# Expert weights laid out by unit, each unit shifted against the moving tiles

## The chip, the cores and the metric

The kernel runs on one core of a Trainium2 chip. The metric is the device time of one execution in microseconds (us). Two runs of the kernel before took 2676.49 and 2677.51 us, median 2677.0. A third execution was profiled; it took 2676.21 us, of which the traced span is 2674.3.

## The reference

Three stages follow each other, all in float32. First, a long convolution: for 2 batches of 12,480 positions and 128 channels, `u = x * v` is convolved along the sequence with a filter that a small network makes from the position embedding (through real FFTs of twice the length), and the result is multiplied by `x`. Its output, 24,960 tokens of 128 channels, then goes through two dense blocks, which the kernel calls experts:

```python
h = x @ w_in                                  # 128 -> 2048
x = (h * np.cos(h)) @ w_out                   # first,  2048 -> 128
h = x @ w_in2
y = (h * np.clip(h + 3, 0, 6) / 6) @ w_out2   # second
```

The expert weights arrive as float64. The kernel decodes each into two float32r numbers, a high and a low part.

## The kernel before, in words

`conv_phase` computes the convolution with two short Fourier transforms as matmuls, in some 530 us. Beside it two `decoder` lanes fetch and decode the expert weights: 16 tasks of 512 columns, four for each of the weight matrices `wi`, `wo` (first expert, in or out) and `vi`, `vo` (second). A task loads 64-bit words by a DMA from SyncE, splits exponent and mantissa on VectorE and ScalarE, writes the high part with a ScalarE copy (L129) and the low part with a GpSimd product (L136). The conv stage calls `step_decode` once in each of its 64 steps, so a task is spread over several steps.

`moe_phase` runs both experts, from about 530 us to the end. Tokens come in 49 tiles of 512 columns (448 in the first and the last). The 2048 hidden channels are cut into 8 units of 256. For each tile and unit:

- `front` (L701 is its operand line, L700 its call) makes the hidden values of one unit: for each of two halves of 128 channels three matmuls are added up in PSUM, high weight by high token, high weight by low token, low weight by high token. These are six matmuls, with one unit's weights as the stationary operand and a token tile (`xh`, `xl`, or `x2h`, `x2l` for the second expert) as the moving one.
- `m1_reduce`, `m1_gate`, `m1_split` (first expert) or `m2_gate`, `m2_split` (second) apply the nonlinearity on ScalarE and VectorE and split the result into `hi` and `lo`; the last subtraction is on GpSimd (L733, L758).
- `back` (L768) multiplies by the output weights, six matmuls again, and adds into `acc`. After the eighth unit `acc` becomes the next expert's token tile or the output.

The loop over `p` at the end of `moe_phase` writes the order out by hand. In its steady part one position issues `front` of the first expert, `back` of the first expert's unit three positions earlier, `front` of the second expert and `back` of its unit three positions earlier: 24 matmuls in four runs of six, each run with the weights of one unit. The units of the four runs differ. `tc.manual_schedule()` keeps this order on every engine. Before the loop 12 matmuls into `busy` (L791) keep TensorE occupied.

Where the tiles lie matters for the change. In the kernel before, a weight tile of the first expert is 128 x 2 x 2048 float32r, all high parts and then all low parts: 16,384 bytes in a partition. A tile of the second expert has `HB` = 4160 elements, 16,640 bytes, since the convolution uses the same place before it. `HB` and `XB` are rounded up to `LINE` = 64 elements, 256 bytes. Moving tiles are 1,792, 2,048 or 4,096 bytes. All of these are multiples of 256 bytes, so every weight tile and every moving tile begins at the same place within 256 bytes, and each stationary block (128 columns, 512 bytes) does too.

Of the kernel before, what the change touches and what calls it, by code (L numbers as in the profile page):

```python
# [9 lines left out]
FP32 = mybir.dt.float32  # L10
F32R = mybir.dt.float32r
# [3 lines left out]
ALU = mybir.AluOpType  # L15
# [13 lines left out]
MP = 2 * M2  # L29
# [4 lines left out]
DFF = 2048  # L34
KFF = DFF // 128
TOK = B * S
TT = 512
XW = 4 * N2
LINE = 64
HB = -(-max(36 * MP, 2 * DFF) // LINE) * LINE  # L40
XB = -(-XW // LINE) * LINE
TILES = [(TT + TOK % TT) // 2] + [TT] * (TOK // TT - 1) + [(TT + TOK % TT) // 2]
TWO_PI = 2.0 * np.pi
# [3 lines left out]
def kernel(  # L47
# [19 lines left out]
    nc = tc.nc  # L67
    dram = ctx.enter_context(tc.tile_pool(name="dram", bufs=1, space=DRAM))
    wp = ctx.enter_context(tc.tile_pool(name="wp", bufs=1))
    scr = dram.tile([D, B, NP1 * N2], FP32, name="scr")  # L70

    w_hi = {}
    w_lo = {}
    DC = 512

    hq = ctx.enter_context(tc.tile_pool(name="hq", bufs=1))

    def weights(e, nm):
        if (nm, e) not in w_hi:
            if e == 0:  # L80
                t = wp.tile([128, 2, DFF], F32R, name=f"w{nm}")
            else:
                t = hq.tile([128, HB], F32R, tag=f"h{'io'.index(nm)}", name=f"v{nm}")[:, :2 * DFF]
                t = t.rearrange("p (z f) -> p z f", f=DFF)
            w_hi[nm, e], w_lo[nm, e] = t[:, 0, :], t[:, 1, :]
        return w_hi[nm, e], w_lo[nm, e]

    b_exp = wp.tile([128, 1], FP32, name="b_exp")
# [9 lines left out]
    def fetch(task, pool, lane):  # L98
# [9 lines left out]
            )  # L108
        return st

    def decode(task, st, pool, lane):
        e, nm, c = task
        lo, hi = st[:, :, 0], st[:, :, 1]
        ex = pool.tile([128, DC], INT32, tag=f"wex{lane}", name="wex")
        mh = pool.tile([128, DC], INT32, tag=f"wmh{lane}", name="wmh")
        m = mh.bitcast(FP32)
        wh, wl = (w[:, c:c + DC] for w in weights(e, nm))
        nc.vector.tensor_scalar(ex, hi, 9, 0x3FFFFF, op0=ALU.logical_shift_right, op1=ALU.bitwise_and)
        nc.vector.tensor_scalar(mh, hi, 0x1FF, None, op0=ALU.bitwise_and)
        yield  # L120
        nc.scalar.activation(out=ex, in_=ex, func=ACTF.Relu, bias=b_exp, scale=-1.0)
        nc.scalar.activation(out=ex, in_=ex, func=ACTF.Relu, bias=b_max, scale=-(2.0 ** 12))
        nc.scalar.activation(out=m, in_=mh, func=ACTF.Copy, scale=2.0 ** -20)
        yield
        nc.vector.scalar_tensor_tensor(
            out=ex, in0=hi, scalar=-0x80000000, in1=ex, op0=ALU.bitwise_and, op1=ALU.bitwise_or
        )
        yield
        nc.scalar.copy(wh, ex.bitcast(FP32))  # L129
        nc.vector.scalar_tensor_tensor(  # L130
            out=m, in0=lo.bitcast(UINT32), scalar=2.0 ** -52, in1=m, op0=ALU.mult, op1=ALU.add
        )
        yield
        nc.vector.tensor_scalar(ex, ex, -0x800000, None, op0=ALU.bitwise_and)
        yield
        nc.gpsimd.tensor_tensor(out=wl, in0=m, in1=ex.bitcast(FP32), op=ALU.mult)  # L136

    LANES = 2
    order = [(0, nm, c) for c in range(0, DFF, DC) for nm in "io"] + [(1, nm, c) for nm in "io" for c in range(0, DFF, DC)]
# [1 line left out]
    def decoder(lane, pool):  # L141
        tasks = order[lane::LANES]
        for _ in range((0, 3)[lane]):
            yield
        st = fetch(tasks[0], pool, lane)
        yield
        for k, task in enumerate(tasks):
            for j, _ in enumerate(decode(task, st, pool, lane)):
                if j == 4 and k + 1 < len(tasks):
                    st = fetch(tasks[k + 1], pool, lane)  # L150
                yield
            yield
# [481 lines left out]
    def moe_phase(mctx):  # L634
# [14 lines left out]
        acc = {}  # L649

        def n_of(t):
            return TILES[t]

        def load_x(t):
            if t >= NT:
                return
            n = n_of(t)
            if t == 0 and n <= XW and _runs(0, n) == [[0, 0, n]]:
                xf[t] = x0_t[t]
                return  # L660
            f = x_p.tile([128, TT], FP32, tag="xf", name="xf")
            done = 0
            for b, p, step in _runs(starts[t], n):
                nc.sync.dma_start(out=f[:, done:done + step], in_=scr[:, b, p:p + step])
                done += step
            xf[t] = f
# [18 lines left out]
        def front(e, t, u, split):  # L685
            n = n_of(t)
            un = Unit()
            un.e, un.t, un.u, un.n = e, t, u, n
            xh, xl = xs[e, t]
            if split:  # L690
                hs = [ps_a.tile([128, 1, TT], FP32, tag=f"ha{c}", name=f"ha{c}") for c in range(2)]
                un.parts = [(slice(c, c + 1), hs[c][:, :, :n]) for c in range(2)]
            else:
                h = ps_b.tile([128, 2, TT], FP32, tag="hb", name="hb")
                hs = [h[:, c:c + 1] for c in range(2)]
                un.parts = [(slice(0, 2), h[:, :, :n])]
            for c in range(2):
                sl = slice((2 * u + c) * 128, (2 * u + c + 1) * 128)
                for k, (w, r) in enumerate(((w_hi, xh), (w_hi, xl), (w_lo, xh))):
                    nc.tensor.matmul(  # L700
                        out=hs[c][:, 0, :n], lhsT=w["i", e][:, sl], rhs=r[:, :n], start=(k == 0), stop=(k == 2)  # L701
                    )
            return un

# [55 lines left out]
        def back(un):  # L760
            e, t, u, n = un.e, un.t, un.u, un.n
            if u == 0:
                bank = 1 if t == 0 else e
                acc[e] = ps_o.tile([128, TT], FP32, tag=f"acc{bank}", name=f"acc{e}")
            for k, (w, r) in enumerate(((w_hi, un.hi), (w_lo, un.hi), (w_hi, un.lo))):
                for c in range(2):
                    sl = slice((2 * u + c) * 128, (2 * u + c + 1) * 128)
                    nc.tensor.matmul(  # L768
                        out=acc[e][:, :n], lhsT=w["o", e][:, sl], rhs=r[:, c, :n],
                        start=(u == 0 and c == 0 and k == 0), stop=(u == KFF // 2 - 1 and c == 1 and k == 2),  # L770
                    )
            if u == KFF // 2 - 1:
                a = acc[e][:, :n]
                if e == 0:
                    hi = x2_p.tile([128, TT], F32R, tag="x2h", name="x2h")
                    lo = x2_p.tile([128, TT], F32R, tag="x2l", name="x2l")
                    nc.scalar.copy(hi[:, :n], a)
                    nc.vector.tensor_tensor(out=lo[:, :n], in0=a, in1=hi[:, :n], op=ALU.subtract)
                    xs[1, t] = (hi, lo)
                else:  # L780
                    o = o_p.tile([128, TT], FP32, tag="o", name="o")
                    nc.scalar.activation(out=o[:, :n], in_=a, func=ACTF.Copy, scale=1.0 / 6.0)
                    nc.sync.dma_start(out=out_t[:, starts[t]:starts[t] + n], in_=o[:, :n])
# [4 lines left out]
        first, second = {}, {}  # L788
        busy = ps_o.tile([128, TT], FP32, tag="acc0", name="busy")
        for _ in range(12):  # L790
            nc.tensor.matmul(out=busy, lhsT=w_hi["i", 0][:, :128], rhs=w_hi["i", 0][:, :TT])  # L791
        load_x(0)
        load_x(1)
        split_x(0)
        for p in range(P2 + 3):
            if p < P1:
                t, u = divmod(p, NU)
                un = first[p] = front(0, t, u, p >= SHIFT or p % 3 == 0)
                un.alone = p < SHIFT
                m1_reduce(un)  # L800
                if u == 3:
                    load_x(t + 2)
                if u == 4:
                    split_x(t + 1)
# [12 lines left out]
            for q in (p - 4, p - 3):  # L817
                if q in first and first[q].alone == (q == p - 4):
                    back(first.pop(q))
            if SHIFT <= p < P2:  # L820
                second[p] = front(1, *divmod(p - SHIFT, NU), p == P2 - 1)
# [9 lines left out]
            if p - 3 in second:  # L831
                back(second.pop(p - 3))

    with tc.manual_schedule():
        nc.gpsimd.memset(b_exp, 1151.0 * 2.0 ** 11 - 1.0)
        nc.gpsimd.memset(b_max, 255.0 * 2.0 ** 23 - 2.0 ** 12)
        nc.gpsimd.memset(b_one, 1.0)
        nc.gpsimd.memset(bias3, 3.0)
        nc.gpsimd.memset(biaspi, float(np.pi / 2))
        nc.gpsimd.memset(biasq, 0.25)  # L840
        with ExitStack() as cctx:
            conv_phase(cctx)
        with ExitStack() as mctx:
            moe_phase(mctx)
# [96 lines left out]
```

## Time and profile before

| | |
|---|---|
| median of two runs | 2677.0 us (2676.49 to 2677.51) |
| profiled execution | 2676.21 us |
| its span | 2674.3 us |
| TensorE busy | 2655.9 us, 99% |
| GpSimd / VectorE / ScalarE busy | 2398.6 / 2343.5 / 2161.2 us |
| mean granted TensorE clock | 0.999 |

Busy time is the union of an engine's instructions. PE is TensorE's matmuls, PEld its weight loads, which run beside matmuls; DVE is VectorE, ACT ScalarE, POOL GpSimd. The end of a matmul is modelled, so its duration in the rows (389 ns for 512 columns) overlaps with the next; the distance from one start to the next is what a matmul takes of the engine.

### The profile page before, as it was taken

The numbers are of one execution on the slowest core, as the hardware profiler recorded it, in microseconds if no ns is written. First come the engines' busy times: TensorE is split into PE (matmuls) and PEld (weight loads), VectorE is DVE, ScalarE is ACT, GpSimd is POOL, SyncE is SP. The second block draws the span as 40 slices with busy tenths as digits, with TensorE's granted clock in tenths as the row PEclk, the third lists the DMA queues.
The fourth block names the chain that finished last, engine by engine and source line by source line (L and its number), as shares of the span: only waits on it lengthen the run. The fifth ranks groups of instructions, "written<-read, shape, count | busy, mean of one in ns | idle before, by whom it ended". The sixth has DMA issues, their size and how long they took to land.

```text
span 2674.3 us, 45722 instructions
## 1 busy us (share of the span) xinstructions
PE 2655.9 (99%) x16362; PEld 2149.8 (80%) x16362; DVE 2343.5 (88%) x3188; ACT 2161.2 (81%) x3140; POOL 2398.6 (90%) x1321
## 2 busy tenths in 40 slices
PE   9999999989999999999999999999999999999999
PEld 6777777678888888888888888888888888888888
DVE  7999998788888888888888888888888888888887
ACT  5666665588888888888888888888888888888885
POOL 6999998789998989898999999898989899999987
PEclk9999999999999999999999999999999999999999
DMA  4443332200000000000000000000000000000000
GB/s 117 108 108 99 103 105 79 64 21 8 17 9 17 17 9 17 9 17 9 16 9 17 9 17 8 17 15 11 16 9 17 9 17 8 17 9 16 8 9 12
DMA packets 88312, 79.86 MB, mean 30 GB/s; under 512 B 57028, under 2 KB 78870, under 8 KB 88086
## 3 DMA queue, kind: packets, MB, share of 16 engines
q1 hardware_dynamic: 87790, 76.80, 10.6%
q8 instruction: 132, 2.16, 0.3%
q14 instruction: 94, 0.77, 0.1%
q10 hardware_dynamic: 296, 0.13, 0.0%
HBM read 51.15 MB, written 25.74 MB: 29 GB/s over the span
## 4 chain that ended last, share of the span: by engine, by line
PE 97%; ACT 1%; POOL 1%; DVE 1%; issue 0%; DMA 0%; SPq 0%; ACTq 0%; DVEq 0%; POOLq 0%
PE acc L768 39%; PE hb L700 20%; PE ha L700 19%; PE ap L281 5%; PE v L281 3%; PE xp L281 3%; PE bp L281 3%; PE xh L281 2%; PE ap L280 1%; PE hps L346 0%; PE bp L280 0%; PE rp L333 0%; ACT r L720 0%; ACT k L710 0%; POOL lo L733 0%
## 5 line engine op out<-in xcount | busy, mean ns | idle before, releaser
L758 POOL TENSOR_TENSOR lo<-g,hi 128x1024 fp32r<-128x1024 f32 (+1 forms) x390 | 938.1, 2406 | 195.4 <-PE ha L700 172.6
L733 POOL TENSOR_TENSOR lo<-g,hi 128x1024 fp32r<-128x1024 f32 (+1 forms) x392 | 941.6, 2403 | 2.8 <-ACT hi L728 2.0
L710 ACT ACTIVATE k<-ha,biasq 128x512 int32<-128x512 f32 (+1 forms) x768 | 501.6, 688 | 264.8 <-PE ha L700 258.5
L721 DVE TENSOR_TENSOR g<-ha,r 128x512 f32<-128x512 f32 (+1 forms) x768 | 499.8, 689 | 230.1 <-ACT r L720 230.0
L700 PE MATMUL hb<-x2h,vi 128*128 128x512 f32 (+1 forms) x1564 | 543.7, 388 | 0.0
L700 PE MATMUL ha<-xh,wi 128*128 128x512 f32 (+1 forms) x1524 | 530.6, 389 | 4.1 <-DVE g L721 4.1
L720 ACT ACTIVATE r<-r,biaspi 128x512 f32<-128x512 f32 (+1 forms) x776 | 520.7, 720 | 0.6 <-DVE r L711 0.4
L711 DVE SCALAR_TENSOR_TENSOR r<-k,ha 128x512 f32<-128x512 int32 (+1 forms) x768 | 488.7, 677 | 2.6 <-ACT k L710 2.3
L741 DVE SCALAR_TENSOR_TENSOR g<-q,hb 128x1024 f32<-128x1024 f32 (+1 forms) x391 | 472.3, 1208 | 7.9 <-ACT q L740 7.8
L755 DVE SCALAR_TENSOR_TENSOR hi<-q,hb 128x1024 fp32r<-128x1024 f32 (+1 forms) x390 | 469.9, 1205 | 0.0
L740 ACT ACTIVATE q<-hb,bias 128x1024 f32<-128x1024 f32 (+1 forms) x391 | 433.5, 1109 | 19.3 <-PE hb L700 18.4
L768 PE MATMUL acc<-hi,wo 128*128 128x512 f32 (+1 forms) x1568 | 418.4, 389 | 0.0
L768 PE MATMUL acc<-hi,vo 128*128 128x512 f32 (+1 forms) x1568 | 417.7, 388 | 0.0
L728 ACT CAST hi<-g 128x1024 fp32r<-128x1024 f32 (+1 forms) x385 | 401.4, 1043 | 0.0
L768 PEld LDWEIGHTS acc<-hi,wo 128*128 128x128 f32 x1568 | 294.8, 188 | 59.9
L768 PEld LDWEIGHTS acc<-hi,vo 128*128 128x128 f32 x1568 | 294.6, 188 | 59.6
L700 PEld LDWEIGHTS hb<-x2h,vi 128*128 128x128 f32 x1564 | 293.3, 188 | 60.2 <-issue 0.6
L700 PEld LDWEIGHTS ha<-xh,wi 128*128 128x128 f32 x1524 | 286.5, 188 | 63.9 <-issue 2.8
L700 PE MATMUL hb<-x2l,vi 128*128 128x512 f32 (+1 forms) x782 | 303.7, 388 | 0.0
L700 PE MATMUL ha<-xl,wi 128*128 128x512 f32 (+1 forms) x762 | 296.1, 389 | 0.0
L768 PE MATMUL acc<-lo,wo 128*128 128x512 f32 (+1 forms) x784 | 241.2, 389 | 0.4 <-DVE g L721 0.3
L768 PE MATMUL acc<-lo,vo 128*128 128x512 f32 (+1 forms) x784 | 240.7, 388 | 0.0
(155 smaller groups left out, 4078.3 us busy)
## 6 DMA issues: line engine op xcount, KB each, us to landing
x<-in_x_dram SPq DMA_DIRECT2D x64, 199.5 KB
v<-in_v_dram SPq DMA_DIRECT2D x64, 199.5 KB
scr<-z SPq DMA_DIRECT2D x128, 98.9 KB
out_dram<-o SPq DMA_DIRECT2D x47, 256.0 KB
xf<-scr SPq DMA_DIRECT2D x17, 256.0 KB
wst<-in_wi_dram SPq DMA_DIRECT2D x8, 512.0 KB
wst<-in_wo_dram SPq DMA_DIRECT2D x8, 512.0 KB
pt<-in_post_dram SPq DMA_DIRECT2D x14, 224.0 KB
```

The costliest lines, as they stand in the source:

```text
L281: nc.tensor.matmul(out=out[OD:m], lhsT=lhsT[:, OD:m], rhs=rhs if rhs2 is None else rhs2)
L700: nc.tensor.matmul(out=hs[c][:, 0, :n], lhsT=w["i", e][:, sl], rhs=r[:, :n], start=(k == 0), stop=(k == 2))
L710: nc.scalar.activation(out=k[:, c, :n], in_=h, func=ACTF.Identity, bias=biasq, scale=1.0 / TWO_PI)
L711: nc.vector.scalar_tensor_tensor(out=un.r[:, c, :n], in0=k[:, c, :n], scalar=-TWO_PI, in1=h, op0=ALU.mult, op1=ALU.add)
L720: nc.scalar.activation(out=rc, in_=rc, func=ACTF.Sin, bias=biaspi, scale=1.0)
L721: nc.vector.tensor_tensor(out=un.g[:, c, :n], in0=h, in1=rc, op=ALU.mult)
L733: nc.gpsimd.tensor_tensor(out=un.lo[:, :, :n], in0=un.g[:, :, :n], in1=un.hi[:, :, :n], op=ALU.subtract)
L740: nc.scalar.activation(out=un.r[:, c, :n], in_=h, func=ACTF.Relu, bias=bias3, scale=1.0)
L741: nc.vector.scalar_tensor_tensor(out=un.g[:, c, :n], in0=un.r[:, c, :n], scalar=6.0, in1=h, op0=ALU.min, op1=ALU.mult)
L755: nc.vector.scalar_tensor_tensor(out=un.hi[:, c, :n], in0=un.r[:, c, :n], scalar=6.0, in1=h, op0=ALU.min, op1=ALU.mult)
L758: nc.gpsimd.tensor_tensor(out=un.lo[:, :, :n], in0=un.g[:, :, :n], in1=un.hi[:, :, :n], op=ALU.subtract)
L768: nc.tensor.matmul(out=acc[e][:, :n], lhsT=w["o", e][:, sl], rhs=r[:, c, :n], start=(u == 0 and c == 0 and k == 0), stop=(u == KFF // 2 - ...
```

## The change

The high and the low part of one unit (256 columns each) now lie side by side, unit after unit, and behind each unit is a gap of `STEP` elements: 2 (8 bytes) for the first expert, 16 (64 bytes) for the second. A unit is 512 elements, 2,048 bytes, and the tiles' starts keep their place within 256 bytes, so unit u's weights begin 8u or 64u bytes past the place of the moving tiles. The matmuls pick the unit by index instead of by column; the decoder writes its 512 columns as two runs of 256. The first expert's tiles grow from 4096 to 4160 elements, the second's from 4160 to 4224.

```diff
 LINE = 64
-HB = -(-max(36 * MP, 2 * DFF) // LINE) * LINE
+UW = 256
+STEP = (2, 16)
+ROOM = [-(-(DFF // UW * (2 * UW + s)) // LINE) * LINE for s in STEP]
+HB = -(-max(36 * MP, ROOM[1]) // LINE) * LINE
...
             if e == 0:
-                t = wp.tile([128, 2, DFF], F32R, name=f"w{nm}")
+                t = wp.tile([128, ROOM[0]], F32R, name=f"w{nm}")
             else:
-                t = hq.tile([128, HB], F32R, tag=f"h{'io'.index(nm)}", name=f"v{nm}")[:, :2 * DFF]
-                t = t.rearrange("p (z f) -> p z f", f=DFF)
-            w_hi[nm, e], w_lo[nm, e] = t[:, 0, :], t[:, 1, :]
+                t = hq.tile([128, HB], F32R, tag=f"h{'io'.index(nm)}", name=f"v{nm}")
+            t = t[:, :DFF // UW * (2 * UW + STEP[e])].rearrange("p (u n) -> p u n", u=DFF // UW)
+            w_hi[nm, e], w_lo[nm, e] = t[:, :, :UW], t[:, :, UW:2 * UW]
...
+    def by_unit(t):
+        return t.rearrange("p (u n) -> p u n", n=UW)
...
-        wh, wl = (w[:, c:c + DC] for w in weights(e, nm))
+        wh, wl = (w[:, c // UW:(c + DC) // UW] for w in weights(e, nm))
...
-        nc.scalar.copy(wh, ex.bitcast(FP32))
+        nc.scalar.copy(wh, by_unit(ex.bitcast(FP32)))
...
-        nc.gpsimd.tensor_tensor(out=wl, in0=m, in1=ex.bitcast(FP32), op=ALU.mult)
+        nc.gpsimd.tensor_tensor(out=wl, in0=by_unit(m), in1=by_unit(ex.bitcast(FP32)), op=ALU.mult)
...
-                sl = slice((2 * u + c) * 128, (2 * u + c + 1) * 128)
+                sl = slice(c * 128, (c + 1) * 128)
...
-                        out=hs[c][:, 0, :n], lhsT=w["i", e][:, sl], rhs=r[:, :n], start=(k == 0), stop=(k == 2)
+                        out=hs[c][:, 0, :n], lhsT=w["i", e][:, u, sl], rhs=r[:, :n], start=(k == 0), stop=(k == 2)
...
-                        out=acc[e][:, :n], lhsT=w["o", e][:, sl], rhs=r[:, c, :n],
+                        out=acc[e][:, :n], lhsT=w["o", e][:, u, sl], rhs=r[:, c, :n],
...
-            nc.tensor.matmul(out=busy, lhsT=w_hi["i", 0][:, :128], rhs=w_hi["i", 0][:, :TT])
+            nc.tensor.matmul(
+                out=by_unit(busy), lhsT=w_hi["i", 0][:, 0, :128], rhs=w_hi["i", 0][:, :TT // UW]
+            )
```

## Rows read from the trace of the kernel before

**Rows 1.** The page: the span, then each engine's busy time, share and instructions.

```profile
span 2674.3 us, 45722 instructions
PE 2655.9 (99%) x16362; PEld 2149.8 (80%) x16362; DVE 2343.5 (88%) x3188; ACT 2161.2 (81%) x3140; POOL 2398.6 (90%) x1321
```

**Rows 2.** The page: the chain that ended last, shares by engine and line.

```profile
PE 97%; ACT 1%; POOL 1%; DVE 1%; issue 0%; DMA 0%; SPq 0%; ACTq 0%; DVEq 0%; POOLq 0%
PE acc L768 39%; PE hb L700 20%; PE ha L700 19%; PE ap L281 5%; PE v L281 3%; PE xp L281 3%; PE bp L281 3%; PE xh L281 2%; PE ap L280 1%; PE hps L346 0%; PE bp L280 0%; PE rp L333 0%; ACT r L720 0%; ACT k L710 0%; POOL lo L733 0%
```

**Rows 3.** Windows by stage: length, busy us (count) per engine, granted clock, DMA.

```profile
core 0: us, PE busy (x) PEld busy (x) DVE busy (x) ACT busy (x) POOL busy (x), PEclk, DMA share, GB/s
100.00:500.00 400.00, 400.00 (x5412) 292.80 (x5410) 353.56 (x590) 251.19 (x499) 372.82 (x355) 1.00 0.38 99
1500.00:2000.00 500.00, 500.00 (x2208) 414.15 (x2207) 443.78 (x564) 433.41 (x587) 452.48 (x196) 1.00 0.05 13
```

**Rows 4.** Timeline of PE and PEld, one position of the steady stage: start, length.

```profile
1500.83 0.39 PE L700 MATMUL hb<-x2h,vi 128*128 128x512 f32 x1
1500.84 0.87 PEld L768 LDWEIGHTS acc<-hi,vo 128*128 128x128 f32 x4
1501.06 1.07 PE L768 MATMUL acc<-hi,vo 128*128 128x512 f32 x4
1501.97 0.61 PE L768 MATMUL acc<-lo,vo 128*128 128x512 f32 x2
1502.42 0.39 PE L700 MATMUL ha<-xh,wi 128*128 128x512 f32 x1
...
1503.78 1.07 PE L768 MATMUL acc<-hi,wo 128*128 128x512 f32 x4
...
1505.14 0.39 PE L700 MATMUL hb<-x2h,vi 128*128 128x512 f32 x1
...
1506.50 0.62 PE L768 MATMUL acc<-hi,vo 128*128 128x512 f32 x2
```

**Rows 5.** Timeline of PE, then the window, where the clock was halved.

```profile
545.29 1.70 PE L768 MATMUL acc<-hi,wo 128*128 128x448 f32 x4
546.79 0.95 PE L768 MATMUL acc<-lo,wo 128*128 128x448 f32 x2
545.30:547.50 2.20, 2.20 (x7) 1.98 (x6) 1.32 (x2) 1.91 (x3) 1.73 (x2) 0.50 0.00 0
```

**Rows 6.** Timeline of PE in the convolution, matmuls of 448 columns in pairs.

```profile
206.97 0.54 PE L281 MATMUL xp<-at,cs 121*49 121x448 f32 x1
...
208.47 0.55 PE L281 MATMUL v<-b,gm 112*48 112x456 f32 x1
```

**Rows 7.** Timeline of PE in the last tiles.

```profile
2650.68 1.09 PE L768 MATMUL acc<-hi,vo 128*128 128x512 f32 x4
2651.60 0.62 PE L768 MATMUL acc<-lo,vo 128*128 128x512 f32 x2
2652.07 0.36 PE L700 MATMUL hb<-x2h,vi 128*128 128x448 f32 x1
...
2653.28 1.09 PE L768 MATMUL acc<-hi,vo 128*128 128x512 f32 x4
2654.21 0.62 PE L768 MATMUL acc<-lo,vo 128*128 128x512 f32 x2
2654.66 0.36 PE L700 MATMUL hb<-x2h,vi 128*128 128x448 f32 x1
```

**Rows 8.** Groups, 1000 to 2500 us: busy us, mean ns | idle before.

```profile
L758 POOL TENSOR_TENSOR lo<-g,hi 128x1024 fp32r<-128x1024 f32 x277 | 669.2, 2416 | 138.7 <-PE ha L700 130.0 <-POOL lo L733 4.8 <-DVE hi L755 2.7
L733 POOL TENSOR_TENSOR lo<-g,hi 128x1024 fp32r<-128x1024 f32 x276 | 666.5, 2415 | 0.2
L768 PEld LDWEIGHTS acc<-hi,wo 128*128 128x128 f32 x1104 | 207.1, 188 | 43.0
L679 POOL TENSOR_TENSOR xl<-xf,xh 128x512 fp32r<-128x512 f32 x35 | 45.6, 1304 | 0.0
```

**Rows 9.** Decoder lines: ns min/median/max, first and last start in us.

```profile
L129 ACT CAST wi<-wex x4: 622/624/626, 69.3 to 207.6; 128x512 fp32r<-128x512 f32 x4
L136 POOL TENSOR_TENSOR wo<-wmh,wex x4: 1299/1302/1307, 108.9 to 247.3; 128x512 fp32r<-128x512 f32 x4
L136 POOL TENSOR_TENSOR vo<-wmh,wex x4: 1292/1300/1312, 361.7 to 431.7; 128x512 fp32r<-128x512 f32 x4
```

**Rows 10.** Timeline of PE at the start of the experts.

```profile
530.17 3.03 PE L791 MATMUL busy<-wi 128*128 128x512 f32 x12
534.76 0.47 PE L700 MATMUL ha<-x0h,wi 128*128 128x448 f32 x1 [1.56 <-ACT x0h L677]
```

More of the change, by code (lines that the diff above doesn't have):

```diff
@@ L766, in back @@
                 for c in range(2):
-                    sl = slice((2 * u + c) * 128, (2 * u + c + 1) * 128)
+                    sl = slice(c * 128, (c + 1) * 128)
                     nc.tensor.matmul(
-                        out=acc[e][:, :n], lhsT=w["o", e][:, sl], rhs=r[:, c, :n],
+                        out=acc[e][:, :n], lhsT=w["o", e][:, u, sl], rhs=r[:, c, :n],
                         start=(u == 0 and c == 0 and k == 0), stop=(u == KFF // 2 - 1 and c == 1 and k == 2),
```

## The prediction

> **What bounds the kernel now.** I read the engines' shares first. TensorE is busy for 2655.9 of 2674.3 us and POOL, the next, for 2398.6 [rows 1]. A busy matmul engine may still be waiting, so the chain of work that ended last is the second view: 97% of it is PE, and 78% lies on two lines, the expert matmuls of L700 and L768 [rows 2]. The windows by stage come third. From 1500 to 2000 us PE has no gap, POOL is busy for 452.5 of 500 us, DVE for 443.8, ACT for 433.4, at full clock [rows 3]. In this stage the end is set by the distance from one matmul's start to the next; nothing else is late.
>
> That distance is in PE's timeline. From 1501.06 to 1506.50 us, one position of the loop, lie 24 matmuls of 512 columns: 5.44 us, 226.7 ns each [rows 4]. The window agrees: 2208 matmuls touch 500 us, some 2206 starts, 226.7 ns. The weight load of a matmul takes 188 ns [rows 8] and begins when the matmul ahead of it begins (load 1500.84, matmul 1500.83 [rows 4]), so it has ended before it is needed. Its length is hidden.
>
> What would a matmul cost without any disturbance? Around 546 us the clock was granted at 0.50 (1.2 GHz), and four matmuls of 448 columns started 545.29 to 546.79 us [rows 5]: 375 ns each by these rounded times, against 448/1.2 = 373.3, one column per cycle. At 2.4 GHz 512 columns are then 213.3 ns. So at full clock each matmul pays 13.3 ns more than its columns, 32 cycles. The convolution's matmuls read each moving column at half that rate: four pairs of 448 columns take 206.97 to 208.47 us, 375 ns a pair, or 376 by the start of each, against 2 x 448/2.4 = 373.3 [rows 6]. They pay 2.7 ns at most, with weights whose two halves lie 452 bytes apart, so off any common line. The surplus therefore belongs to full-rate reading of moving data beside a weight load, and I take 13.3 - 2.7 = 10.6 ns as the part that a collision in memory could explain.
>
> That part is not constant. In the last tiles, where matmuls of 448 columns break the rhythm, six of 512 columns, on the same tiles and tags, take 2650.68 to 2652.07 = 1.39 us, and 2653.28 to 2654.66 = 1.38 us; in the steady stage six take 1.36 us (1501.06 to 1502.42) [rows 4, 7]. The steady stage holds a regular pitch, better than a disturbed one by 20 to 30 ns per run of six.
>
> **The change, part by part.** No instruction, DMA, wait or queue entry is added, removed or moved. The work is 49 tiles x 8 units x 24 = 9408 expert matmuls, 1568 runs of six that share one unit's weights, 784 for each expert.
>
> (a) Tile sizes. Each weight tile grows by 256 bytes, 64 elements; every later tile moves by a multiple of 256 bytes. Before, all weight and moving tiles stand at the same place within 256 bytes, since all are multiples of that. Unit 0 keeps that place. Cost nothing; the last tile moves up by 1 KB.
>
> (b) The weight decoder writes its 512 columns as two runs of 256. There are 16 ACT copies of 0.62 us and 16 POOL products of 1.3 us [rows 9], between 69 and 433 us, where PE is busy for 400 of 400 us and POOL for 373 [rows 3]. If a second run cost 10% of each, 16 x 0.19 = 3 us would fall on engines with over 27 us to spare in that stage. The first expert's last product starts at 247.3 [rows 9], 283 us before the first matmul that reads these weights at 530.17 [rows 10]. Zero; 3 us if that cover failed.
>
> (c) The 12 warm-up matmuls read their moving columns as two runs. They start at 530.17 and take 3.03 us [rows 10]; PE then waits until 534.76 for the first token tile [rows 10]. Zero.
>
> (d) The shift itself: weights of unit u begin 8u bytes (first expert) or 64u bytes (second) past the place that the moving tiles have. No row shows such a shift, so it is bounded from both sides. Below: all of the 10.6 ns goes for the 7 units of 8 that are shifted, 8232 x 10.6 = 87 us less. Above: the collisions double, 87 us more. The nearest rows lie between and near zero. For whole steps of 256 bytes the trace has a case: the second expert's output weights stand 16,640 bytes behind its input weights, 32.5 x 512, so 256 bytes apart within 512, while the moving tiles all keep one place; yet L700 on vi and L768 on vo have the same pitch [rows 4]. Moving whole lines did nothing there, so for the 64-byte steps I take nothing. For the 8-byte steps I take the disturbed rhythm: each run of six has another shift than the run ahead of it, and starts out of step, 25 ns dearer. 784 x 25 ns = 20 us.
>
> Sum: 2676.2 (the profiled execution) + 20 = 2696; the median of the runs shown is 0.8 us above that execution, so **2697 us**. Own range of this case: from 2677 (the runs fall back into step at once) to 2677 + 1568 x 30 ns = 2724 (both experts out of step).
>
> If matmuls got cheaper, POOL would be next: 2.416 + 2.415 + 1.304/8 = 4.99 us per position [rows 8], against 24 x 216.1 = 5.19 for PE. So a gain on PE would reach the end in full.
>
> **A rule against it.** The rows show 226.7 ns at full clock. The Trainium skill, page "SBUF — State Buffer", in the section on the two sides and its table of paths, gives TensorE its own ports, with a second independent one for weight loads, and says that PE never waits on anyone. By it places in memory could not matter, and the sum would be 2677. The page "TensorE: Matmul & The Clock Gate" (section "Wait — 56ns, not 53.3ns?") puts a warm matmul of 512 columns at 215.7 ns; this trace does not agree, with 226.7.
>
> **Rivals.**
> *Nothing changes* (chance 0.24): 2677 us. The surplus is a property of loading and streaming, not of addresses, or the pitch falls back into step after one matmul. For it: the same pitch on vi and vo, and no surplus that follows the weights' place in the convolution [rows 4, 6]. Against: the pitch of one shape is not fixed [rows 7]. The port rule cited above would make this outcome.
>
> *The collisions thin out* (0.22): today every load begins at the very place where its moving tile begins, the worst start if both streams step through the same banks side by side. Shifted units would escape. For it: the surplus exists only at the full rate of 4 bytes per cycle [rows 4 to 6]. Against: no run of six in the rows is below 1.36 us, in step or out of it [rows 4, 7]. All of it gives 2677 - 87 = 2590 us; one expert alone, 2677 - 44 = 2633. It passes 2% when the mean pitch drops by 53.5 us/9408 = 5.7 ns, to 221.0. I give 0.16 to that and 0.06 to less.
>
> *The collisions double* (0.14): shifted loads no longer share line boundaries with the moving stream, so each line they touch disturbs two. The mean pitch would have to pass 232.4 ns to be slower by 2%; the dearest run in the rows is 1.39/6 = 231.7 [rows 7], which speaks against. All shifted matmuls at twice the surplus: 2677 + 87 = 2764 us. Over 2%: 0.13.
>
> **The numbers.** The forecast has 0.40. The likeliest time is 2697. About 2% is what a measurement of this kernel can be told from no change by here. Faster by more: 0.16. Slower by more: 0.13. Within: 0.40 + 0.24 + 0.06 + 0.01 = 0.71. The range for 8 in 10 runs from 2600 (leaving some 0.07 of the thinning case out) to 2730 (leaving out the doubling, 0.13). Both signs hold a good part, so the forecast's own range, 2677 to 2724, stands beside it.
>
> **What would show it.** Unit u of every run can be read from the order of the matmuls, so the profile after gives a pitch for each shift. The forecast says: L768 on vo and L700 on vi at 226 to 228 ns, L700 on wi and L768 on wo at 229 to 232, the first matmuls of each run dearest, PE without gaps, the convolution's 530 us as before. All four at 226.7: nothing changes. A pitch near 216 for some units: thinning. Over 233: doubling. Any PE gap on a weight tile, or a convolution longer than 533 us, would make parts (b) and (c) wrong.

## The result, and the profile after

The changed kernel takes 2715.5 us in the median of two runs (2715.19 and 2715.86) against 2677.0: a ratio of 1.0144, 95% interval 1.0100 to 1.0188. It is slower by 38.5 us, inside the stated range (2600 to 2730), on the forecast's side, and about twice as far from the old time as the 20 us that were forecast.

The page of the changed kernel, its span, engines and chain, answers to [rows 1, 2]. L706 and L774 are the lines that were L700 and L768.

```profile
span 2714.1 us, 45722 instructions
PE 2696.1 (99%) x16362; PEld 2153.5 (79%) x16362; DVE 2344.7 (86%) x3188; ACT 2176.2 (80%) x3140; POOL 2405.9 (89%) x1321
PE 97%; ACT 1%; POOL 1%; DMA 1%; DVE 0%; issue 0%; SPq 0%; ACTq 0%; POOLq 0%; DVEq 0%
```

The counts are those of before. PE's busy time grew by 40.2 us, the span by 39.8; DVE, POOL and ACT grew by 1.2, 7.3 and 15.0. The windows of the changed kernel, in the columns of [rows 3], say where:

```profile
100.00:500.00 400.00, 400.00 (x5412) 292.79 (x5410) 353.83 (x589) 251.36 (x499) 372.80 (x356) 1.00 0.38 99
1500.00:2000.00 500.00, 500.00 (x2166) 407.03 (x2165) 436.02 (x553) 429.70 (x577) 448.05 (x193) 1.00 0.05 12
```

In the convolution PE has the same 5412 matmuls in the same 400 us. In the expert stage PE has no gap and full clock, as before, but 2166 matmuls where 2208 stood: 500 us / 2164 starts = 231.05 ns instead of 226.7. 4.4 ns x 9408 matmuls = 41 us. So TensorE waits for no other engine here; each matmul holds it longer.

The chain of the changed kernel, read in order of time, gives one piece per run of six matmuls: start us, length us, line.

```profile
717.21 1.41 PE ha L706 x6
718.62 1.39 PE acc L774 x6
720.01 1.38 PE hb L706 x6
721.39 1.36 PE acc L774 x6
722.75 1.36 PE ha L706 x6
724.11 1.36 PE acc L774 x6
725.47 1.36 PE hb L706 x6
726.83 1.40 PE acc L774 x6
728.22 1.39 PE ha L706 x6
729.61 1.39 PE acc L774 x6
```

The unit of each run follows from the order of the loop. The shifts are, from top to bottom, 56 bytes (`wi`), 32 (`wo`), 192 (`vi`), 0 (`vo`), 0 (`wi`), 40 (`wo`), 256 (`vi`), 64 (`vo`), 8 (`wi`), 48 (`wo`). The three runs at 0 or 256 bytes and the one at 40 take the old 1.36 us; the others 1.38 to 1.41. Over the stretch from 700 to 2500 us I averaged the starts of all runs of each shift, six matmuls in ns:

```
first expert   shift     0     8    16    24    32    40    48    56
  wi                  1360  1382  1398  1380  1391  1406  1400  1407   mean 1390
  wo                  1380  1389  1400  1387  1396  1360  1393  1395   mean 1388
second expert  shift mod 256   0    64   128   192
  vi                        1365  1395  1394  1374                     mean 1382
  vo                        1364  1398  1399  1375                     mean 1384
```

Against 1360, and with 392 runs of each kind, the first expert lost 392 x (30 + 28) ns = 23 us and the second 392 x (22 + 24) ns = 18 us. Together 41 us, against 39.65 us between the two profiled executions (2715.86 and 2676.21).

### The profile page after: what moved, and what is told of

It is laid out like the page before. It is cut to its first block, busy times and chain, and to the rows that moved or that the text cites. A ratio compares the mean times of both kernels' runs of the same rounds, so it can differ in the third digit from the quotient of the medians.

```text
span 2714.1 us, 45722 instructions
## 1 busy us (share of the span) xinstructions
PE 2696.1 (99%) x16362; PEld 2153.5 (79%) x16362; DVE 2344.7 (86%) x3188; ACT 2176.2 (80%) x3140; POOL 2405.9 (89%) x1321
## 4 chain that ended last, share of the span: by engine, by line
PE 97%; ACT 1%; POOL 1%; DMA 1%; DVE 0%; issue 0%; SPq 0%; ACTq 0%; POOLq 0%; DVEq 0%
PE acc L774 39%; PE hb L706 20%; PE ha L706 19%; PE ap L287 5%; PE v L287 3%; PE xp L287 3%; PE bp L287 3%; PE xh L287 2%; PE ap L286 1%; PE hps L352 0%; PE bp L286 0%; PE rp L339 0%; ACT r L726 0%; DMA x<-scr 0%; POOL lo L739 0%; ACT k L716 0%
## 5 line engine op out<-in xcount | busy, mean ns | idle before, releaser
L764 POOL TENSOR_TENSOR lo<-g,hi 128x1024 fp32r<-128x1024 f32 (+1 forms) x390 | 939.5, 2409 | 226.7 <-PE ha L706 147.0
L716 ACT ACTIVATE k<-ha,biasq 128x512 int32<-128x512 f32 (+1 forms) x768 | 507.6, 688 | 287.1 <-PE ha L706 287.1
L706 PE MATMUL hb<-x2h,vi 128*128 128x512 f32 (+1 forms) x1564 | 548.0, 391 | 0.0
L706 PE MATMUL ha<-xh,wi 128*128 128x512 f32 (+1 forms) x1524 | 538.7, 394 | 3.0 <-DVE g L727 3.0
L774 PE MATMUL acc<-hi,wo 128*128 128x512 f32 (+1 forms) x1568 | 426.1, 394 | 0.0
L774 PE MATMUL acc<-hi,vo 128*128 128x512 f32 (+1 forms) x1568 | 422.8, 391 | 0.0
L774 PEld LDWEIGHTS acc<-hi,wo 128*128 128x128 f32 x1568 | 296.4, 189 | 67.2
L706 PEld LDWEIGHTS hb<-x2h,vi 128*128 128x128 f32 x1564 | 293.9, 188 | 67.1 <-issue 0.4
L774 PEld LDWEIGHTS acc<-hi,vo 128*128 128x128 f32 x1568 | 294.6, 188 | 63.6
L706 PEld LDWEIGHTS ha<-xh,wi 128*128 128x128 f32 x1524 | 287.1, 188 | 69.3 <-issue 2.9
L706 PE MATMUL hb<-x2l,vi 128*128 128x512 f32 (+1 forms) x782 | 307.1, 393 | 0.0
L706 PE MATMUL ha<-xl,wi 128*128 128x512 f32 (+1 forms) x762 | 300.0, 394 | 0.0
L774 PE MATMUL acc<-lo,wo 128*128 128x512 f32 (+1 forms) x784 | 243.9, 392 | 0.5 <-DVE g L727 0.3
L774 PE MATMUL acc<-lo,vo 128*128 128x512 f32 (+1 forms) x784 | 244.2, 393 | 0.0
```

The source lines that it names most:

```text
L706: nc.tensor.matmul(out=hs[c][:, 0, :n], lhsT=w["i", e][:, u, sl], rhs=r[:, :n], start=(k == 0), stop=(k == 2))
L716: nc.scalar.activation(out=k[:, c, :n], in_=h, func=ACTF.Identity, bias=biasq, scale=1.0 / TWO_PI)
L764: nc.gpsimd.tensor_tensor(out=un.lo[:, :, :n], in0=un.g[:, :, :n], in1=un.hi[:, :, :n], op=ALU.subtract)
L774: nc.tensor.matmul(out=acc[e][:, :n], lhsT=w["o", e][:, u, sl], rhs=r[:, c, :n], start=(u == 0 and c == 0 and k == 0), stop=(u == KFF // 2 ...
```

## The experiments

Two theories stood after the result. *Out of step* (A) was the forecast's: a run of six pays because its shift differs from that of the run ahead, and would pay nothing if all runs had the same shift. *Place* (B): the distance between the start of the weights and the start of the moving columns sets a pitch (the time from one matmul's start to the next) of its own, whatever went before. A third (C) was that the layout costs, not the shift. The times of the kernel before, run on the same chips beside the kernels that are timed below, had medians of 2676.85 to 2677.3 us.

**The layout alone.**

```diff
-STEP = (2, 16)
+STEP = (0, 0)
```

> The by-unit layout without any shift (both steps 0). Theory A (out of step: the loss comes from runs of six whose shift differs from the run ahead) and theory B (place: each shift has a pitch of its own, whatever stood before it) both expect the time of the kernel before, 2677 us within 3 us, and 226.7 ns from matmul to matmul. Theory C (the layout itself costs: two runs in the decoder, hi and lo parts 1 KB apart instead of 8 KB) expects all or most of the 38.5 us, 2700 to 2716 us.

Measured: 2677.4 us, ratio 1.0001 (0.9992 to 1.0010). One window, in the columns of [rows 3], holds the 2208 matmuls of before:

```profile
1500.00:2000.00 500.00, 500.00 (x2208) 414.01 (x2207) 444.41 (x564) 433.39 (x586) 452.29 (x195) 1.00 0.04 12
```

C falls: the decoder's writing in two pieces and the high part lying beside the low part cost nothing.

**One expert at a time.**

```diff
-STEP = (2, 16)
+STEP = (2, 0)      # "first";  (0, 16) in "second"
```

> Only the first expert is shifted, 8 bytes per unit; the second stays at the place of the moving tiles. From the trace of the changed kernel the first expert's matmuls cost some 4.9 ns more on average and the second's 3.9. Theory B expects 4704 x 4.9 = 23 us more, 2700 us, with the second expert's runs at 226.7 to 228. Theory A expects 1568 runs that each follow a run with another shift, so also a loss on the second expert's runs: 2677 + 784 x 25 ns for each expert, 2716 us at most and 2697 at least. The forecast had 2697 for this step.

> Only the second expert is shifted, 64 bytes per unit. The forecast took nothing for this step: 2677 us. Theory B, from the pitches in the changed kernel (64 and 128 bytes about 233, 192 bytes 229, 0 and 256 bytes 226.7): 4704 x 3.9 = 18 us more, 2695 us.

Measured: first 2700.9 us, ratio 1.0090 (1.0075 to 1.0105); second 2699.9 us, 1.0087 (1.0070 to 1.0103). The shift of the first expert alone costs 24 us, that of the second alone 23, and both together 38.5, less than the sum. Place expected 2700 and 2695, the forecast 2697 and 2677. So the 64-byte steps, which the forecast took at nothing, cost as much as the 8-byte steps. The unshifted expert does not come off free, though. In the chain of the kernel with only the first expert shifted:

```profile
735.25 1.40 PE hb L706 x6
736.65 1.38 PE acc L774 x6
738.02 1.39 PE ha L706 x6
739.41 1.36 PE acc L774 x6
740.77 1.36 PE hb L706 x6
```

The first two rows are `vi` and `vo`, at shift 0, behind a run of `wo` with 56 bytes; they pay 1.40 and 1.38. The last is `vi` again, behind an unshifted run, with 1.36. On average the unshifted `vi` took 1373 ns and `vo` 1366, so a run out of the rhythm does pay something. Over 392 runs of each that is 392 x (13 + 6) ns = 7 us of the 24; in the kernel with only the second expert shifted the unshifted `wi` took 1374 ns and `wo` 1361, 392 x (14 + 1) ns = 6 us of the 23. This is what is true of A. The starts in the trace show it as a settling: the six matmuls of `vi` above lie 237, 233, 236, 224, 231 and 236 ns apart, those of `vo` behind them 228, 233, 231, 226, 227 and 231. A stream at shift 0 that starts afresh (`saa` in the kernel with all shifts below) goes through nearly the same series, 235, 233, 236, 224, 231, 236, 228, 232, 231, before it stays at 226.7.

**One shift for all.**

```diff
-STEP = (2, 16)
+STEP = (0, 0)
+BASE = 16
...
-            t = t[:, :DFF // UW * (2 * UW + STEP[e])].rearrange("p (u n) -> p u n", u=DFF // UW)
+            t = t[:, BASE:BASE + DFF // UW * (2 * UW + STEP[e])].rearrange("p (u n) -> p u n", u=DFF // UW)
```

> No step between units; all weights of both experts begin 64 bytes past the place of the moving tiles. No run of six differs in shift from the run ahead of it. Theory A expects the rhythm to hold: 226.7 ns and 2677 us. Theory B expects the two-beat of the 64-byte units of the changed kernel (235.8 and 230.8 ns, mean 233.3) everywhere: 9408 x 6.6 ns = 62 us more, 2739 us.

Measured: 2736.4 us, ratio 1.0222 (1.0207 to 1.0237). The chain of this kernel:

```profile
1500.00 1.40 PE hb L707 x6
1501.40 1.40 PE acc L775 x6
1502.80 1.40 PE ha L707 x6
1504.20 1.40 PE acc L775 x6
```

Every run of the steady stage takes 1.40 us, 233.3 ns a matmul, with no change of shift anywhere. A, which had 2677, falls; B had 2739.

**All shifts, as streams.** To see the pitch of every shift in its steady state, streams of equal matmuls were put where the 12 warm-up matmuls stand, in the kernel before.

```diff
+        def stream(name, shift, cols=128, n=TT, at=0, count=36):
+            b = ps_o.tile([128, TT], FP32, tag="acc0", name=name)
+            a = at + 1024 + shift // 4
+            for _ in range(count):
+                nc.tensor.matmul(
+                    out=b[:cols, :n], lhsT=w_hi["i", 0][:, a:a + cols], rhs=w_hi["i", 0][:, at:at + n]
+                )
...
```

> The kernel before, with streams of 36 equal matmuls added where the 12 warm-up matmuls stand; their results are read by nobody. In each stream the weights begin a constant number of bytes past the place of the moving columns, 0 to 252 in steps of 4, up and then down again with both operands 64 bytes further on; then both moved together by 64 and by 20 bytes, streams with 64 or 32 weight columns instead of 128, and with 448 or 256 moving columns instead of 512. Theory B (place): a stream at 0 runs at 226.7 ns, at 64 and 128 bytes at 233.3, at 192 at 228.9, the same on the way down, and moving both operands together changes nothing; if the surplus of 32 cycles comes from weight reads in the way of moving reads, half the weight columns give about half the surplus, 220 ns, and a quarter 217. Theory A (out of step): every stream settles at 226.7 ns whatever its shift. Theory D (the surplus belongs to the matmul and not to its weight load): 226.7 ns with 64 and 32 weight columns too.

In the timeline of this kernel (start us, length us) each stream is one row: `saa` has shift 0, `sca` 64, `seb` 132 bytes; `pa`, `pb` have shift 0 with both operands 64 and 20 bytes further on; `ca` and `cc` have 64 and 32 weight columns; `na`, `nb` and `nc`, `nd` have 448 and 256 moving columns with shift 0 and 64.

```profile
532.67 8.49 PE L797 MATMUL saa<-wi 128*128 128x512 f32 x36
...
671.86 8.67 PE L797 MATMUL sca<-wi 128*128 128x512 f32 x36
...
819.74 8.45 PE L797 MATMUL seb<-wi 128*128 128x512 f32 x36
...
1645.76 8.49 PE L797 MATMUL pa<-wi 128*128 128x512 f32 x36
1654.31 8.73 PE L797 MATMUL pb<-wi 128*128 128x512 f32 x36
...
1671.83 8.50 PE L797 MATMUL ca<-wi 128*64 128x512 f32 x36
...
1689.02 8.52 PE L797 MATMUL cc<-wi 128*32 128x512 f32 x36
1697.59 7.70 PE L797 MATMUL na<-wi 128*128 128x448 f32 x36
1705.35 7.55 PE L797 MATMUL nb<-wi 128*128 128x448 f32 x36
1712.96 4.58 PE L797 MATMUL nc<-wi 128*128 128x256 f32 x36
1717.59 4.38 PE L797 MATMUL nd<-wi 128*128 128x256 f32 x36
```

A stream's length holds a slow start and the modelled end, so I took the mean distance between starts from the seventh matmul on, on the way up (first row) and on the way down (second row, with both operands 64 bytes further on):

```
shift   0     40     64     120    128    132    156    164    192    240
ns     227.5  233.5  233.3  226.7  232.7  226.7  226.7  237.6  229.0  228.3
ns     226.7  233.3  233.3  226.7  232.4  227.1  243.6  237.6  229.0  226.7
```

Of the 64 shifts 33 (up) and 29 (down) lie between 233.0 and 233.6; the mean of all is 232.5. None is below 226.65. Shift 0 is among the five that reach 226.7 at least one way, with 120, 132, 156 and 240. A, which expected 226.7 everywhere, falls a second time. Four expectations of my own failed as well. At 12, 60, 100, 116 and 156 bytes the way down gave a pitch 3 ns or more away from the way up, and moving both operands by 20 bytes changed it too (234.9), so the distance between the two is not all. With fewer weight columns the surplus (what a matmul takes beyond its columns) did not halve: 230.0 ns with 64 and 231.8 with 32, against 226.7 with 128. So at this length it does not go with the amount of weight data read; but with D (a cost of the matmul alone) it would have stayed at 226.7. And shift 0 is not the best at every length: for 256 columns shift 64 is better (113.3 against 120.0 ns). For 448 columns it was so here as well (202.1 against 206.7), but the next kernel did not repeat that.

**Lengths.** The same streams with other moving lengths:

```diff
...
+        for i in range(17):
+            for j, shift in enumerate((0, 64, 120, 132, 192, 240)):
+                stream("n" + ab[i] + ab[j], shift, n=512 - 8 * i, count=30)
+        for j, at in enumerate((1, 2, 4, 8, 16)):
+            stream("p" + ab[j], 0, at=at)
+        for j, cols in enumerate((96, 64, 32)):
+            stream("c" + ab[j], 0, cols=cols, n=480)
```

> Streams of equal matmuls again, now with 512 down to 384 moving columns in steps of 8, each with the weights 0, 64, 120, 132, 192 and 240 bytes past the place of the moving columns; then both operands moved together by 4, 8, 16, 32 and 64 bytes, and 480 columns with 96, 64 and 32 weight columns. If a stream settles on a beat of 16 cycles (6.67 ns) that depends on place and length together, the pitch at shift 0 is a multiple of 16 cycles for many lengths, and the surplus over the columns swings between 16 and 48 cycles with the length: 32 at 512 and 256, 48 at 448 as seen. A length of 480 or 496 at 496 or 512 cycles (206.7 or 213.3 ns) would then be the best use of TensorE. If the surplus is one fixed cost per matmul at shift 0, every length shows 32 cycles. Moving both operands by 16, 32 or 64 bytes should keep 226.7 ns if only the relative place matters; by 20 bytes it was 234.9, so 4 and 8 bytes may not.

Measured, in cycles of 2.4 GHz above the number of columns (granted clock 1.00; from the sixth matmul on), at the six shifts in that order, for six of the 17 lengths:

```
columns   0     64    120   132   192   240
512      34.3  48.0  32.0  32.0  37.3  36.0
496      40.0  48.0  42.6  32.0  48.0  33.1
480      40.0  38.2  58.0  40.0  44.0  40.0
448      38.0  37.3  48.0  48.0  32.0  32.0
424      32.0  24.0  40.0  43.1  40.1  40.0
384      33.0  32.0  32.0  40.0  32.0  32.0
```

(512 at shift 0 still holds a few matmuls on the way to 32.) The hoped-for 16 cycles at 480 or 496 are not there: over all 17 lengths the surplus lies between 24 and 58, most often on 32, 40 or 48. At 448 columns and shift 0 this kernel has 38 cycles, 202.5 ns, where the one before had 206.7 with the same operands; what differs is what ran before. Per column no length beats 512 at 544 cycles by more than 424 at shift 64 does, 448 against 450.5 cycles for 424 columns, 0.6%. Together moved by 32 and 64 bytes the pair kept its pitch (545.7 and 546.0 cycles, start included), by 4, 8 and 16 bytes it did not (570.6, 554.7, 560.0). With 480 moving columns at shift 0 the weight columns acted the other way than with 512; in the timeline the streams `ca`, `cb` and `cc` have 96, 64 and 32 of them:

```profile
1231.32 8.11 PE L797 MATMUL ca<-wi 128*96 128x480 f32 x36
1239.48 8.02 PE L797 MATMUL cb<-wi 128*64 128x480 f32 x36
1247.55 7.88 PE L797 MATMUL cc<-wi 128*32 128x480 f32 x36
```

Their steady pitch is 524, 520 and 512 cycles, against 520 with 128 weight columns.

**Two more constant shifts, and other places of the moving columns.** The edit is that of 64 bytes with `BASE = 30` and `48`; the streams are those of above with `at` from 1 to 7 elements and 32 shifts each.

> All weights 120 bytes past the place of the moving tiles, no step between units. The streams at 120 bytes settled at 226.66 ns, up and down. If the steady pitch of each shift, as the streams show it, is what the kernel pays, this one costs nothing: 2677 us within 5. If any shift off the line costs what 64 bytes cost, 2737 us.

> All weights 192 bytes past the place of the moving tiles. The streams gave 229.0 ns, the units with 192 bytes in the changed kernel 228.8 to 229.5. Place theory: 9408 x 2.3 ns = 21 us more, 2698 us. Any shift costs the same: 2737 us.

> Streams of 512 columns with the moving columns themselves 4 to 28 bytes past the place of the kernel's tiles, each with the weights 0 to 248 bytes further in steps of 8. If 544 cycles (226.7 ns) is the least that any pair of places gives, no stream is below it and the kernel before stands at the best place; a stream at 528 cycles (220 ns) would point to a version faster than both, 9408 x 6.7 = 63 us less.

Measured: 120 bytes 2677.7 us, ratio 1.0003 (0.9993 to 1.0012); 192 bytes 2695.9 us, 1.0069 (1.0052 to 1.0086). The streams foretold both, 2677 and 2698. The chain of the kernel with 120 bytes, start and length of each run of six:

```profile
1500.97 1.36 PE hb L707 x6
1502.33 1.36 PE acc L775 x6
```

The chain of the kernel with 192 bytes, 1.37 us a run:

```profile
1501.08 1.37 PE ha L707 x6
1502.45 1.37 PE acc L775 x6
```

The 224 streams at other places of the moving columns ran at 544 to 576 cycles. None was faster than the 544 cycles of the kernel before.

**Change without a bad place, and a bad place without change.** Input weights at 0 and output weights at 120 bytes; and all weights at 40 bytes (`BASE = 10`). The edit of the first is shown against the kernel with 120 bytes.

```diff
-BASE = 30
+BASE = {'i': 0, 'o': 30}
...
-            t = t[:, BASE:BASE + DFF // UW * (2 * UW + STEP[e])].rearrange("p (u n) -> p u n", u=DFF // UW)
+            t = t[:, BASE[nm]:BASE[nm] + DFF // UW * (2 * UW + STEP[e])].rearrange("p (u n) -> p u n", u=DFF // UW)
```

> Input weights at the place of the moving tiles, output weights 120 bytes past it. Both shifts alone give 2677 us, and every run of six now has another shift than the run ahead. What remains is the price of changing between two good places. Out of step at each change, as the forecast priced it: 1568 x 25 ns = 39 us more, 2716 us. Place alone: 2677 us. In the kernel with only the first expert shifted, the unshifted runs behind a shifted one took 1366 and 1373 ns instead of 1360: by that, up to 1568 x 10 ns = 16 us more, 2693 us.

> All weights 40 bytes past the place of the moving tiles. The streams at 40 bytes settled at 233.4 ns; units with 40 bytes whose neighbours run in step held 226.7 ns in the changed kernel and in the one with only the first expert shifted. If the pitch depends on the place alone, 9408 x 6.7 ns = 63 us more, 2740 us. If a shift can hold either of two rhythms, by how it was entered, 2677 or 2740 us, and a trace that switches between 1360 and 1400 ns per run after an interruption.

Measured: alternating 2676.6 us, ratio 0.9999 (0.9989 to 1.0008); 40 bytes 2736.1 us, 1.0222 (1.0205 to 1.0239). The chain of the alternating kernel, whose rows change their shift each time:

```profile
1501.02 1.36 PE acc L775 x6
1502.38 1.36 PE hb L707 x6
1503.74 1.36 PE acc L775 x6
```

The chain of the kernel with 40 bytes everywhere:

```profile
1500.45 1.40 PE acc L775 x6
1501.85 1.40 PE ha L707 x6
```

A change of shift at every run costs nothing with these two shifts, each of which holds 1.36 us by itself. And 40 bytes, which held 1.36 us for a run of six between unshifted runs in the changed kernel (724.11 above), stays at 1.40 when all weights have it. It is not alone in this: `wo` at 16 bytes took 1400 ns in the changed kernel and 1360 in the one with only the first expert shifted. So the place alone does not fix a run's length; the runs ahead have a part in it.

## Why the prediction was right in its range and wrong in a step

**What bounds the kernel**: right. The pitch of the expert matmuls sets the end; PE stayed without gaps, and 4.4 ns per matmul appear in the span in full.

**Parts (a), (b), (c)**: right. The layout without shift gave 2677.4. The convolution's window holds the same 5412 matmuls.

**Part (d), the first expert**: the size was right, 20 us forecast against 23 in the changed kernel's trace and 24 by itself. The reason was not. "Each run of six has another shift than the run ahead of it, and starts out of step" is refuted as the main cause twice: 64 bytes everywhere, no change at all, costs 59.6 us; 0 and 120 bytes in turn, a change at every run, cost nothing. Nor were the first matmuls of a run the dearest, as the forecast said: averaged by place in the run, the first matmul of `wi` takes 231.0 ns and the others 231.1 to 232.6; on `wo` it takes 232.0 and the others 230.7 to 231.7. The disturbed runs of [rows 7] stand at shift 0 behind matmuls of 448 columns; their 25 ns are no price of a place, and that the shifted places of the first expert cost 20 to 47 ns a run (0 at 40 bytes) is near it by luck.

The streams' pitches come close to the changed kernel's time. Averaged over the units' shifts they lie 5.17 ns above 226.7 for the first expert and 3.72 for the second: 4704 x 5.17 ns = 24.3 us and 4704 x 3.72 ns = 17.5 us, together 41.8 against 38.5 measured. For one expert alone, though, 24.3 and 17.5 stand against 24 and 23 measured, and where the first matches, its trace divides it otherwise: the shifted expert's own runs lost 18 us and the unshifted one's 7. How much of the 38.5 us is place and how much is settling after a change is not shown.

**Part (d), the second expert**: this is the step that failed. "Moving whole lines did nothing there, so for the 64-byte steps I take nothing" carried a case of 256 bytes over to 64. The 256 bytes were read rightly: `vi` at a shift that is a multiple of 256 takes 1365 ns in the changed kernel, near the old 1360. But within those 256 bytes 64 and 128 cost 34 to 39 ns a run and 192 some 14. That term was 18 us beside the other expert, 23 us alone, instead of 0. The forecast's signs for it, 226 to 228 ns on `vi` and `vo`, came out at 230.4 and 230.7. It is nearly the whole of what the sum of 2697 us lacked. The upper end of the forecast's own range, 2724, had priced it at 30 ns a run.

**The rivals.** *Nothing changes* is refuted. The same instructions take 226.7 or 233.3 ns by where their operands lie. The Trainium skill, in the page "SBUF — State Buffer" (section "SBUF: two separate sides"), gives weight loads an independent port and says that TensorE never waits on anyone. From that the prediction had drawn that places could not matter, and the measurement decides otherwise. No stream of 512 columns and 128 weight columns ran below 226.7 ns. That is far from the 215.7 ns that the Trainium skill gives in the page "TensorE: Matmul & The Clock Gate" (section "Wait — 56ns, not 53.3ns?"). *Thinning* is refuted for the places tried: the kernel before already stands at the least pitch found. *Doubling* is refuted in size: it meant 237.3 ns, and the dearest run of the changed kernel took 1407/6 = 234.5. Some streams did reach it (237.6 at 164 bytes, 243.6 at 156 one way), at shifts that the change does not use.

**Open**: why the places matter. The runs show that the surplus depends on the places of both operands, on the length and on what ran before, and that fewer weight columns raise it with 512 moving columns (32 cycles with 128, 44 with 32) and can lower it with 480 (40 cycles with 128, 32 with 32). At half the clock and in the convolution it was nearly absent [rows 5, 6], but only one place each was seen there, and the convolution's matmuls differ in more than their rate. The mechanism is not shown. No version faster than the kernel before was found among these places and lengths.

## What to carry to other kernels

When TensorE has no gap and its float32r matmuls still take longer than their columns, the byte addresses of the stationary and the moving operand are a parameter: look at the distance between starts, not at the busy share, and compare it between operands with different places. A null result for one distance (256 bytes) says nothing of the distances inside it. Before reshaping a layout, put a few streams of equal matmuls at the candidate places into the kernel; here some 8 us of stream per place foretold kernels with one shift for all weights to 4 us. With shifts that change from run to run it is a first estimate only.

## What the runs showed of the hardware that was not expected

With float32r operands, a granted clock of 1.00 (2.4 GHz), 512 moving columns and 128 weight columns, a matmul's steady pitch was 226.7 ns (544 cycles) at its best places and 233.3 ns (560 cycles) at about half of the 64 shifts within 256 bytes. At shift 0 a stream took some ten matmuls to settle, longer than one of the kernel's runs of six. In the kernels with one shift for all weights the distances fall into a rhythm that repeats after a few matmuls: 235.8 and 230.8 ns in turn at 64 bytes, 231.7, 225.8 and 229.2 at 192. The sums of these two rounds are whole multiples of 6.67 ns (466.7 and 686.7), 16 cycles. At 40 bytes two pitches were seen: 233.3 ns in streams and in a whole kernel, 226.7 for a run of six between unshifted runs. With 256 columns the shift of 64 bytes was the better one, 113.3 against 120.0 ns.
